# Seven-product query and key projections, whole PSUM bank pairs for turned tiles, weight sums on GpSimd, and a new order

## The chip, the cores and the metric

The kernel runs on one core of one Trainium2 chip. The metric is device time in microseconds, the lower the better. The engines are TensorE (PE), VectorE (DVE), ScalarE (ACT), GpSimd (POOL) and SyncE (SP); PEld is PE's weight load. All transfers are issued by SP.

## What is computed

Three layers follow each other, for B = 2 batches of S = 768 tokens, all in fp32:

```python
# 1. retention, 8 heads of 64
state = gamma * state + k_t v_t^T;  y_t = scale * q_t state
# 2. MLP on x = [y of all heads], 512 wide
xn = (x - mean) / sqrt(var + 1e-6) * g_ln
x = x + relu(xn @ w_ch1) @ w_ch2          # 512 -> 2048 -> 512
# 3. attention of 4 experts, head size 64, two of them chosen by token
logits = x @ w_gate; weights = softmax over the top 2
q, k, v = x @ wq[e], x @ wk[e], x @ wv[e]
out += weight[e] * (softmax(causal(scale * q k^T)) @ v @ wo[e])
```

## The kernel before

One program holds all three layers. Every step is a node with an engine (or several to choose from), a cost, and the buffers that it reads and writes. A planner in the kernel's own code (`Plan.issue`) simulates the engines with those costs, gives each buffer its place in SBUF or PSUM when its first step starts, and writes the instructions in the order so found. Where several steps are ready, the one with the lowest number goes first: the place in the code, a bias, and a value from a table (`RANK`). The names of the table are the labels set by `P.at`, such as "q_proj 1". So costs, ranks and buffer places together decide the order on each engine, and each engine then works its list in order.

The retention runs in 12 tiles of 128 tokens (`r_tile`, L581 to L669): scores on PE (L581), the mask on DVE (L587), the products with the values and the running state (L600, L610), the update of the state (L618), a turn by PE transposes (L422), mean and variance on DVE (L642), the normalised tile xn on ACT (L655), a second turn, and a split of x into a rounded part and a residue, of which the sum is the fp32 value. A matrix product is then three products: high by high, high by residue, residue by high. Weights come as 64-bit floats in pieces (`load_piece`), which ACT, POOL and DVE turn into two parts (`split_piece`, L685 to L719).

The MLP has 8 layers of 256 channels, called f. The first two take twelve matmuls of 128x384 for a channel block and 384 tokens (`m_h`, L766), the later six seven products instead of eight for a block of two by two (`m_h7`, L858). These need sums of weights (`w_sums`, L735 and L740) and of tokens (`x_sums`, L817 to L827), all split into two parts again. `m_c` (L788) multiplies with the second matrix and adds to xT on DVE (L794); its last layer writes x once more as high part and residue (L801, L804).

The attention begins with queries and keys (`q_proj`, L952: twelve matmuls for each of batch, token block j, matrix and half p), values and gates (`q_val`, L976). `a_scores` makes scores (L1047), mask and maximum (L1054), exponentials (L1062), the division (L1068, L1069) and, on POOL, the gated weights (L1076). `a_turn` transposes them by PE (L422) into PSUM and copies them out on ACT or DVE (L446), `a_value` multiplies with the values (L1117), `a_out` with wo (L1144).

PSUM has eight banks of 512 words. A turned tile lies in two neighbouring banks, half in each, and two turned tiles share such a pair: `pb` names six places in three pairs for the retention, `pc` four places in two pairs for the attention. Fillers (L529) are matmuls on constants that stand at the start, where PE would be idle.

## Time and profile before

| | |
|---|---|
| median of 3 runs | 443.25 us (442.27 to 444.95) |
| the profiled execution's own time | 442.45 us |
| its span in the trace | 440.7 us |
| granted PE clock, mean | 0.999 |

A busy share is the time in which an engine has an instruction in work, over the span or a stretch. A row of waits says for whose instruction an engine stood idle. Matmuls overlap, so a matmul's mean duration is longer than its pitch, the time from one start to the next.

### The profile page before, as it was taken

To read this page: it belongs to the slowest core of one execution; us is meant where nothing else is said; L and a number is where in the kernel's file an instruction comes from. 1 tells how busy PE (TensorE), PEld (TensorE's weight loads), DVE (VectorE), ACT (ScalarE), POOL (GpSimd) and SP (SyncE) were. 2 spreads that over 40 slices of the span, in tenths; PEclk is the share of its full clock that TensorE was granted. 3 is DMA by queue.
4 is the path that set the end of the run, shared out by engine and by line. 5 is a ranking of instruction groups with operands and counts; after the bars stand their busy time and mean duration, and the time that the engine had idled before them with its cause. 6 is when DMAs were issued, how large, how long until landed. Compare 5 with 4: busy or idle time off the path is not lost.

```text
span 440.7 us, 9076 instructions
## 1 busy us (share of the span) xinstructions
PE 429.4 (97%) x3546; PEld 402.4 (91%) x3546; DVE 309.8 (70%) x743; ACT 217.7 (49%) x460; POOL 212.0 (48%) x219
## 2 busy tenths in 40 slices
PE   9988999999999999999999999999999999999996
PEld 8877889999999999999999999999999877887765
DVE  2769978765778876868877655668556778667663
ACT  1568775342656346335353264234533666656552
POOL 2668865999999528117136054200401343422430
PEclk9999999999999999999999999999999999999999
DMA  8999432210322304104112002001100001001121
GB/s 288 328 337 345 133 109 84 97 49 1 106 86 92 101 0 143 50 1 136 54 59 88 1 1 96 1 0 55 48 1 1 1 12 39 2 0 49 50 97 49
DMA packets 11995, 35.18 MB, mean 80 GB/s; under 512 B 1840, under 2 KB 2480, under 8 KB 11952
## 3 DMA queue, kind: packets, MB, share of 16 engines
q1 hardware_dynamic: 11952, 34.60, 22.7%
q8 instruction: 28, 0.46, 0.4%
q14 instruction: 15, 0.12, 0.1%
HBM read 31.45 MB, written 3.15 MB: 79 GB/s over the span
## 4 chain that ended last, share of the span: by engine, by line
PE 90%; ACT 3%; DVE 2%; DMA 2%; POOL 1%; issue 1%; SPq 0%; POOLq 0%; DVEq 0%
PE ps L788 30%; PE ps L858 20%; PE ps L766 8%; PE ps L952 8%; PE ps L1117 4%; PE ps L976 4%; PE ps L422 4%; PE ps L1144 4%; PE ps L1047 3%; DMA raw<-in_w_dram 2%; PE ps L529 2%; PE ps L610 1%; PE ps L581 1%; ACT xn L655 1%; PE ps L600 1%
## 5 line engine op out<-in xcount | busy, mean ns | idle before, releaser
L788 PE MATMUL ps<-h,w 128*128 128x384 f32 x768 | 142.4, 335 | 0.0
L788 PEld LDWEIGHTS ps<-h,w 128*128 128x128 f32 x768 | 133.7, 188 | 0.7 <-DVE ps L798 0.3
L794 DVE TENSOR_TENSOR xT<-xT,ps 128x384 f32<-128x384 f32 x112 | 60.2, 550 | 30.6 <-PE ps L788 30.1
L1076 POOL TENSOR_SCALAR pr<-pr,sm,gate 128x384 f32<-128x384 f32 (+5 forms) x48 | 34.0, 718 | 77.9 <-DVE sm L1069 34.1
L719 POOL TENSOR_TENSOR w<-wy,w 128x512 fp32r<-128x512 f32 x26 | 34.0, 1319 | 38.1 <-PE ps L788 23.4
L858 PE MATMUL ps<-t,S 128*128 128x384 f32 x216 | 42.1, 334 | 0.0
L858 PEld LDWEIGHTS ps<-t,S 128*128 128x128 f32 x216 | 37.8, 188 | 0.0
L1062 ACT ACTIVATE pr<-pr,sm 128x384 f32<-128x384 f32 (+5 forms) x48 | 31.7, 663 | 9.9 <-DVE sm L1054 9.9
L766 PE MATMUL ps<-x,w 128*128 128x384 f32 x192 | 35.2, 337 | 0.0
L877 ACT ACTIVATE h<-ps 128x384 fp32r<-128x384 f32 x36 | 17.7, 490 | 32.9 <-PE ps L788 20.6
L766 PEld LDWEIGHTS ps<-x,w 128*128 128x128 f32 x192 | 33.2, 188 | 0.3
L685 ACT ACTIVATE wx<-raw 128x512 f32<-128x512 f32 x32 | 21.5, 671 | 23.8 <-DVE ps L692 16.0
L687 POOL TENSOR_SCALAR wx<-wx 128x512 f32<-128x512 f32 x32 | 20.0, 625 | 23.9 <-ACT wx L685 23.0
L867 ACT ACTIVATE u<-ps 128x384 f32<-128x384 f32 x36 | 17.5, 488 | 25.3 <-PE ps L858 16.6
L858 PE MATMUL ps<-x,w 128*128 128x384 f32 x144 | 28.6, 334 | 0.0
L689 DVE TENSOR_SCALAR ps<-wx 128x512 uint32<-128x512 uint32 x32 | 22.0, 688 | 6.4 <-POOL wx L687 6.1
L858 PEld LDWEIGHTS ps<-x,w 128*128 128x128 f32 x144 | 25.3, 188 | 0.0
L1054 DVE CUSTOM_DVE_ANT_0 pr<-ps,mask 128x384 f32<-128x384 f32 (+4 forms) x48 | 22.1, 495 | 3.2 <-PE ps L1047 2.2
L695 DVE SCALAR_TENSOR_TENSOR wy<-raw,ps 128x512 uint32<-128x512 uint32 x32 | 21.8, 683 | 2.3 <-POOL w L719 1.7
L879 DVE SCALAR_TENSOR_TENSOR h<-ps,h 128x384 fp32r<-128x384 f32 x36 | 19.4, 551 | 5.3 <-ACT h L877 5.2
L692 DVE SCALAR_TENSOR_TENSOR ps<-wx,ps 128x512 uint32<-128x512 uint32 x32 | 22.2, 695 | 1.1
L587 DVE TENSOR_TENSOR am<-ps,caus 128x512 f32<-128x512 f32 x24 | 15.5, 683 | 9.9 <-PE ps L581 9.9
(122 smaller groups left out, 822.7 us busy)
## 6 DMA issues: line engine op xcount, KB each, us to landing
raw<-in_w_dram SPq DMA_DIRECT2D x32, 512.0 KB, 3.4
kq<-in_kq_dram SPq DMA_DIRECT2D x11, 512.0 KB, 5.1
vk<-in_vk_dram SPq DMA_DIRECT2D x9, 512.0 KB, 5.5
out_dram<-ob SPq DMA_DIRECT2D x11, 256.0 KB, 2.0
vk<-in_vk_dram SPq DMA_DIRECT2D x4, 256.0 KB, 3.8
vraw<-in_wv_dram SPq DMA_DIRECT2D x1, 520.0 KB, 3.9
kq<-in_kq_dram SPq DMA_DIRECT2D x2, 256.0 KB, 5.2
mraw<-in_wk_dram SPq DMA_DIRECT2D x1, 512.0 KB, 4.6
```

Source lines behind the costliest of these rows:

```text
L689: DVE(0.69, lambda: dve.tensor_scalar(u32(z), u32(x), 4, 1, op0=OP.logical_shift_left, op1=OP.logical_shift_right), r=[x], w=[z])
L692: DVE(0.7, lambda: dve.scalar_tensor_tensor(u32(z), u32(x), 0x80000000, u32(z), op0=OP.bitwise_and, op1=OP.bitwise_or), r=[x, z], w=[z])
L695: DVE(0.7, lambda: dve.scalar_tensor_tensor(u32(y), words(0), 29, u32(z), op0=OP.logical_shift_right, op1=OP.bitwise_or), r=[raw, z], w=[y])
L719: POOL(1.3, lambda: pool.tensor_tensor(f32r(l), f32(y), f32(h), OP.subtract), r=[y, h], w=[l])
L766: pe.matmul(f32(pa, TB), lhsT=wt, rhs=blk(f32r(xt[b][j]))[:, k], start=(n == 0), stop=(n == 11))
L788: pe.matmul(f32(pa, TB), lhsT=wt, rhs=t, start=(n == 0), stop=(n == 5))
L794: DVE(0.55, lambda: dve.tensor_tensor(blk(f32(xt))[:, k], blk(f32(xt))[:, k], f32(pa, TB), OP.add), r=[pa] + [(xt, cc, w) for cc in range( ...
L858: pe.matmul(f32(pa, TB), lhsT=wt, rhs=t, start=(first and n == 0), stop=(n == 5), skip_group_check=True)
L952: pe.matmul(f32(pa, TB), lhsT=mw(n, lo, k, p * 128, (p + 1) * 128), rhs=blk(f32r(xt))[:, k], start=(i == 0), stop=(i == 11))
L1054: DVE(0.22 + wide * 1.04e-3, lambda ks=ks, n=n, z=z, SC=SC: dve.tensor_tensor_reduce(f32(PR[z])[:, ks], f32(SC[z])[:, :wide], f32(MASK)[:, ...
L1062: ACT(act_c(nk) + .18, lambda pr=pr, z=z: act.activation(f32(pr, nk), f32(pr, nk), AF.Exp, bias=f32(sm)[:, z:z + 1], scale=-1.0, accum_out ...
L1076: POOL(0.34 + nk * 0.84e-3, lambda pr=pr, z=z, e=e: pool.tensor_scalar(f32(pr, nk), f32(pr, nk), f32(sm)[:, 6 + z:7 + z], GT[b, j][:, cc, ...
```

## The change

- `pb` and `pc` now give a turned tile a whole pair of banks: three places for the retention, four for the attention (all eight banks). In the attention a tile holds up to six blocks instead of four. Scores and values may use all banks.
- The queries and keys of a batch are made by seven products of six matmuls instead of eight (`q_proj(b, n)`), as `m_h7` does. That takes sums of the blocks of wk and wq on POOL (`load_mw`), differences of token blocks, which POOL makes a second time with the final x (`x_sums(b, False)`), and steps that keep and add products (ACT, DVE). `m_c` copies the final x to xT for it (ACT).
- `w_sums` may no longer take DVE. The division's addition is done in two steps of one column.
- The running states of both batches count as one thing, so an update waits for the copy of the other batch's state too.
- Some regions of SBUF move (batch 0's queries, keys and values, the probability tiles), and every rank and some costs change.

```diff
-    "q_proj 1": (32, (-66, -79, -22, 88, -127, 8, 130, 119)),
+    "q_proj 1": (28, (-88, -100, -69, -116, -49, -91, -74, -142)),
...
-    PL["psa"] = banks[4:][::-1]
-    PL["ps1"] = banks[:4]
+    PL["psa"] = banks[::-1]
+    PL["ps1"] = banks
     PL["state"] = banks[:1]
 
...
-    PL["pb"] = [("P", 1024 * i + 256 * k, 256) for i in (1, 2, 3) for k in range(2)]
-    PL["pc"] = [("P", 1024 * i + 256 * k, 256) for i in (3, 2) for k in range(2)]
-
-    def two(b):
-        i, k = divmod(b.at[1], 1024)
-        return ps[:, 1024 * i:1024 * i + 1024].rearrange("p (h c) -> p h c", h=2)[:, :, k:k + 256]
+    PL["pb"] = [("P", 1024 * i, 1024) for i in (1, 2, 3)]
+    PL["pc"] = [("P", 1024 * i, 1024) for i in (3, 2, 1, 0)]
+
+    def two(b, n=256):
+        return view(b).rearrange("p (h c) -> p h c", h=2)[:, :, :n]
 
...
-            PE(0.47, upd, form="columns", r=[(vk, 1), vs] + (["first"] if i == 1 else []), w=[(STATE, b)] + (["first"] if i == 0 else []))
+            PE(0.47, upd, form="columns", r=[(vk, 1), vs], w=[STATE])
...
-            P.add({"V": 1.5, "G": 0.76} if f < ALONE else {"G": 0.75}, lambda e, i=i, p=p, q=q, op=op: (dve if e == "V" else pool).tensor_tensor(
+            P.add({"G": 0.75}, lambda e, i=i, p=p, q=q, op=op: (dve if e == "V" else pool).tensor_tensor(
...
         P.at = "m_c 5"
+        ACT(0.49, lambda: act.activation(blk(f32(xt))[:, k], f32(pa, TB), AF.Copy), r=[pa], w=[(xt, "k", k)])
+        P.at = "m_c 6"
         DVE(0.55, lambda: dve.tensor_tensor(blk(f32r(xl))[:, k], f32(pa, TB), blk(f32(xh))[:, k], OP.subtract),
-            r=[pa, (xh, "k", k)], w=[(xl, "k", k)] + (keys(xl) if k == 0 else []))
+            r=[pa, (xt, "k", k), (xh, "k", k)], w=[(xl, "k", k)] + (keys(xl) if k == 0 else []))
 
...
-    def x_sums(b):
+    def x_sums(b, own=True):
...
+        xs = {2: (0, 1), 0: (0, 0), 1: (1, 1), 3: (1, 0)}
+
+        def part(t, new):
+            if own or new:
+                return lambda: plain(tl[t]), [tl[t]]
+            kh, j = xs[t]
+            return lambda: f32(XT[b][j])[:, kh * TW:(kh + 1) * TW], [(XT[b][j], "k", 2 * kh + k) for k in range(2)]
+
+        for t, p, q, made in ((0, 2, 0, ()), (2, 1, 2, ()), (1, 1, 0, (0,)), (3, 3, 1, (1,))):
+            (xp, rp), (xq, rq) = part(p, p in made), part(q, q in made)
             P.at = "x_sums 2"
-            both(lambda en, t=t, p=p, q=q: en.tensor_tensor(plain(tl[t]), plain(tl[p]), plain(tl[q]), OP.subtract),
-                 [tl[p], tl[q]], [tl[t]])
+            both(lambda en, t=t, xp=xp, xq=xq: en.tensor_tensor(plain(tl[t]), xp(), xq(), OP.subtract), rp + rq, [tl[t]])
...
+        if n in ("wk", "wq"):
+            sh, sl = new("Sq"), new("Sq")
+            at = lambda i, m: f32(raw)[:, 512 * i:512 * i + 512].rearrange("p (k m c) -> p k m c", k=2, m=2)[:, :, m]
+            part = lambda i: plain(sl)[:, 256 * i:256 * i + 256].rearrange("p (k c) -> p k c", k=2)
+            for i, p, q, op in ((0, lambda: at(0, 1), lambda: at(1, 1), OP.add),
+                                (1, lambda: part(0), lambda: at(0, 0), OP.subtract),
+                                (2, lambda: at(0, 0), lambda: at(0, 1), OP.subtract),
+                                (3, lambda: at(1, 0), lambda: part(1), OP.subtract)):
+                P.at = "load_mw 4"
+                POOL(0.76, lambda i=i, p=p, q=q, op=op: pool.tensor_tensor(part(i), p(), q(), op), r=[raw], w=[sl])
+            P.at = "load_mw 5"
+            ACT(1.1, lambda: act.activation(f32r(sh), plain(sl), AF.Copy), r=[sl], w=[sh])
+            P.at = "load_mw 6"
+            POOL(2.41, lambda: pool.tensor_tensor(f32r(sl), plain(sl), f32(sh), OP.subtract), r=[sl, sh], w=[sl])
+            MW[n, "S"] = (sh, sl)
...
-    def q_proj(b, j, n, p):
-        cs = slice(j * TB, (j + 1) * TB)
-        pa = new("ps")
-        xh, xl = XH[b][j], XL[b][j]
-        for hf in range(2):
-            def mm(hf=hf):
-                i = 6 * hf
-                for k in (2 * hf, 2 * hf + 1):
-                    for lo, xt in ((0, xh), (0, xl), (1, xh)):
-                        pe.matmul(f32(pa, TB), lhsT=mw(n, lo, k, p * 128, (p + 1) * 128), rhs=blk(f32r(xt))[:, k],
-                                  start=(i == 0), stop=(i == 11))
+    def q_proj(b, n):
+        sh, sl = MW[n, "S"]
+
+        def product(pa, wn, xn, first):
+            h, l = (sh, sl) if wn[0] == "s" else MW[n][:2]
+            c0, step = (256 * int(wn[1]), 128) if wn[0] == "s" else ((512 if wn[0] == "y" else 0) + 128 * int(wn[1]), 256)
+            if xn[0] == "t":
+                xs = TH[b][int(xn[1])], TL[b][int(xn[1])]
+                xr, xat = list(xs), lambda k: tuple(f32r(t)[:, k * TB:(k + 1) * TB] for t in xs)
+            else:
+                kh, xs = int(xn[1]), (XH[b][int(xn[2])], XL[b][int(xn[2])])
+                xr, xat = xkeys(xs[0]) + xkeys(xs[1]), lambda k: tuple(blk(f32r(t))[:, 2 * kh + k] for t in xs)
+
+            def mm():
+                i = 0
+                for k in range(2):
+                    wh, wl = (f32r(t)[:, c0 + k * step:c0 + k * step + 128] for t in (h, l))
+                    xh, xl = xat(k)
+                    for wt, t in ((wh, xh), (wh, xl), (wl, xh)):
+                        pe.matmul(f32(pa, TB), lhsT=wt, rhs=t, start=(first and i == 0), stop=(i == 5), skip_group_check=True)
                         i += 1
             P.at = "q_proj 1"
-            PE(1.06, mm, r=list(MW[n][:2]) + xkeys(xh) + xkeys(xl) + ["seven"], w=[pa])
-        hi, lo = (QK[n, y, b, p] for y in range(2))
-        by = 0.125 if n == "wq" else 1.0
-        P.at = "q_proj 2"
-        ACT(0.485, lambda: act.activation(f32r(hi)[:, cs], f32(pa, TB), AF.Copy, scale=by), r=[pa], w=[(hi, j)])
-        P.at = "q_proj 3"
-        DVE(0.556, lambda: dve.scalar_tensor_tensor(f32r(lo)[:, cs], f32(pa, TB), by, f32(hi)[:, cs], op0=OP.mult, op1=OP.subtract),
-            r=[pa, (hi, j)], w=[(lo, j)])
+            PE(1.04, mm, r=[h, l] + xr + ["seven"], w=[pa])
+
+        def keep(pa):
+            u = new("uq")
+            P.at = "q_proj 2"
+            ACT(0.49, lambda: act.activation(f32(u), f32(pa, TB), AF.Copy), r=[pa], w=[u])
+            return u
+
+        def add(dst, pa, u):
+            P.at = "q_proj 3"
+            DVE(0.55, lambda: dve.tensor_tensor(f32(dst, TB), f32(pa, TB), f32(u), OP.add), r=[pa, u], w=[dst])
+
+        def out(src, p, j):
+            cs = slice(j * TB, (j + 1) * TB)
+            hi, lo = (QK[n, y, b, p] for y in range(2))
+            by = 0.125 if n == "wq" else 1.0
+            P.at = "q_proj 4"
+            ACT(0.485, lambda: act.activation(f32r(hi)[:, cs], f32(src, TB), AF.Copy, scale=by), r=[src], w=[(hi, j)])
+            P.at = "q_proj 5"
+            DVE(0.556, lambda: dve.scalar_tensor_tensor(f32r(lo)[:, cs], f32(src, TB), by, f32(hi)[:, cs], op0=OP.mult, op1=OP.subtract),
+                r=[src, (hi, j)], w=[(lo, j)])
+
+        pa, pb, pc = (new("ps") for _ in range(3))
+        product(pa, "a0", "x00", True)
+        c1 = keep(pa)
+        product(pb, "s1", "t1", True)
+        add(pb, pb, c1)
+        product(pa, "y0", "x10", False)
+        out(pa, 0, 0)
+        u2 = keep(pb)
+        product(pc, "s0", "t0", True)
+        product(pb, "s2", "t2", False)
+        u3 = keep(pb)
+        c22 = new("uq")
+        add(c22, pc, u3)
+        product(pb, "y1", "t3", False)
+        out(pb, 1, 0)
+        product(pc, "s3", "x11", False)
+        add(pc, pc, u2)
+        out(pc, 0, 1)
+        out(c22, 1, 1)
...
-            dve.tensor_scalar(m[:, 4:6], m[:, 2:4], 1e-9, None, op0=OP.add)
+            for z in range(2):
+                dve.tensor_scalar(m[:, 4 + z:5 + z], m[:, 2 + z:3 + z], 1e-9, None, op0=OP.add)
...
-            for s0 in range(0, len(slots), 4):
-                part = slots[s0:s0 + 4]
+            half = (len(slots) + 1) // 2 if len(slots) > 4 else len(slots)
+            for s0 in range(0, len(slots), half):
+                part = slots[s0:s0 + half]
...
+    x_sums(0, False)
     flush()
+    x_sums(1, False)
 
     def q_phase(b):
         q_alloc(b)
         for j in range(NB):
-            for n in ("wk", "wq"):
-                for p in range(2):
-                    q_proj(b, j, n, p)
-            P.bias += 20 * (b + 1)
             for t in range(TPB):
                 q_val(b, TPB * j + t)
             gates(b, j)
-            P.bias -= 20 * (b + 1)
+        for n in ("wk", "wq"):
+            q_proj(b, n)
```

By the orders, the 192 matmuls of L952 become 168 (L995), and 48 copies of turned probability tiles 40. PE has 2296 rows before and 2273 now, DVE 668 and 670, ACT 379 and 421, POOL 224 and 256.

Below stand three places of the order. Numbers in names are buffers and differ between the two programs; line numbers after the change are higher by 8 to 78.

POOL ahead of the projections, before: the residues of four weight matrices, then the first gated probabilities.

```order
L925 TENSOR_TENSOR wk_3218<-mraw_3176,wk_3208 128x1024
L925 TENSOR_TENSOR wq_3242<-mraw_3192,wq_3227 128x1024
L925 TENSOR_TENSOR wo_3565<-mraw_3518,wo_3555 128x1024
L925 TENSOR_TENSOR wv_3585<-vraw_3507,wv_3539 128x1040
L1219 MEMSET mask_3611 128x640
L1076 TENSOR_SCALAR pr_3641<-pr_3641,sm_3642,gate_72 128x384
```

And now: the differences of token blocks of batch 0 (t from xT), their residues (t from t, t), and batch 1's first ones, among the residues of wo and wv.

```order
L840 TENSOR_TENSOR t_1304<-xT_616,xT_140 128x768
L840 TENSOR_TENSOR t_1335<-xT_616,t_1304 128x768
L840 TENSOR_TENSOR t_1384<-xT_140,t_1335 128x768
L840 TENSOR_TENSOR t_1258<-xT_616 128x768
L845 TENSOR_TENSOR t_1453<-t_1304,t_1386 128x768
L845 TENSOR_TENSOR t_1469<-t_1335,t_1402 128x768
L845 TENSOR_TENSOR t_1443<-t_1384,t_1428 128x768
L840 TENSOR_TENSOR t_1502<-xT_764,xT_248 128x768
L845 TENSOR_TENSOR t_1425<-t_1258,t_1407 128x768
L943 TENSOR_TENSOR wo_3666<-mraw_3556,wo_3598 128x1024
L840 TENSOR_TENSOR t_1484<-xT_764 128x768
L943 TENSOR_TENSOR wv_3711<-vraw_3543,wv_3588 128x1040
```

Ten POOL steps now stand where the residues of wo and wv stood alone, and the products with sums on PE follow them.

POOL ahead of the first seven-product layer (f = 2), before: residues of weight pieces (L719, L710), token sums (L817, L821), one weight sum (L735) and the residue of the weight sums (L740).

```order
L817 TENSOR_TENSOR t_1579<-x_363,x_389 128x768
L710 TENSOR_TENSOR w_218_1595<-wy_1571,w_218_1595 128x256
L735 TENSOR_TENSOR sf_1604<-wy_1571 128x256
L719 TENSOR_TENSOR w_225_1625<-wy_1581,w_220_1601 128x512
L687 TENSOR_SCALAR wx_1627<-wx_1627 128x512
L817 TENSOR_TENSOR t_1639<-x_933,x_957 128x768
L821 TENSOR_TENSOR t_1579<-t_1518,t_1579 128x768
L740 TENSOR_TENSOR S_1677<-sf_1604,S_1665 128x1024
```

And now, up to the same residue (L748):

```order
L827 TENSOR_TENSOR t_1611<-x_389,x_407 128x768
L718 TENSOR_TENSOR w_222_1615<-wy_1593,w_222_1615 128x256
L743 TENSOR_TENSOR sf_1632<-wy_1593,wy_1613 128x256
L743 TENSOR_TENSOR sf_1632<-sf_1632,wy_1593 128x256
L743 TENSOR_TENSOR sf_1632<-wy_1593 128x256
L743 TENSOR_TENSOR sf_1632<-wy_1613,sf_1632 128x256
L695 TENSOR_SCALAR wx_1650<-wx_1650 128x512
L840 TENSOR_TENSOR t_1611<-t_1611,t_1529 128x768
L748 TENSOR_TENSOR S_1697<-sf_1632,S_1676 128x1024
```

All four weight sums (L743) now stand on POOL; before, three of them stood on DVE. From the first token sum to this residue POOL has 27 steps before and 33 now, 16 and 20 of them token sums.

SP at the start, before (kq holds a tile's keys and queries, vk its values and keys):

```order
L505 DMA vk_82<-in_vk_dram 128x512
L495 DMA kq_85<-in_kq_dram 128x1024
L495 DMA kq_90<-in_kq_dram 128x512 x2
L498 DMA tabV<-in_tabV_dram 128x48
L500 DMA caus<-in_caus_dram 128x128
L505 DMA vk_98<-in_vk_dram 128x1024
L513 DMA tab_5_103<-in_tabY_dram 128x512
L505 DMA vk_82<-in_vk_dram 128x512
L505 DMA vk_126<-in_vk_dram 128x1024
L515 DMA decay<-in_decay_dram 128x24
```

And now:

```order
L503 DMA kq_82<-in_kq_dram 128x512
L523 DMA decay<-in_decay_dram 128x24
L508 DMA caus<-in_caus_dram 128x128
L503 DMA kq_82<-in_kq_dram 128x512
L506 DMA tabV<-in_tabV_dram 128x48
L521 DMA tab_2_91<-in_tabY_dram 128x512
L548 DMA ident<-in_ident_dram 128x128
L513 DMA vk_96<-in_vk_dram 128x512
L552 DMA gln<-in_gln_dram 128x4
L503 DMA kq_103<-in_kq_dram 128x1024
L513 DMA vk_116<-in_vk_dram 128x1024
L513 DMA vk_96<-in_vk_dram 128x512
```

The first tile's keys and queries (kq_82, in two halves) now come first, tables between them, its values (vk_96) eighth. Before, the values of that tile came first and the keys of two tiles next.

## Rows read from the trace of the kernel before

**Rows 1.** The page: the span, and each engine's busy time, share and instructions.
```profile
span 440.7 us, 9076 instructions
PE 429.4 (97%) x3546; PEld 402.4 (91%) x3546; DVE 309.8 (70%) x743; ACT 217.7 (49%) x460; POOL 212.0 (48%) x219
```

**Rows 2.** Busy us by stage: PE, PEld, DVE, ACT, POOL; granted clock, DMA share, GB/s.
```profile
0.00:7.00 7.00, 5.95 (x30) 5.83 (x30) 0.17 (x2) 1.28 (x1) 0.20 (x4) 1.00 0.72 228
7.00:62.00 55.00, 51.10 (x879) 44.44 (x880) 43.68 (x99) 35.16 (x73) 40.39 (x50) 1.00 0.76 269
62.00:146.00 84.00, 84.00 (x536) 82.85 (x533) 62.93 (x118) 41.99 (x77) 76.39 (x61) 1.00 0.22 75
146.00:312.00 166.00, 166.00 (x958) 165.78 (x958) 119.14 (x217) 73.44 (x141) 55.57 (x55) 1.00 0.17 55
312.00:338.00 26.00, 26.00 (x176) 25.25 (x174) 15.26 (x54) 8.67 (x21) 6.77 (x5) 1.00 0.01 3
338.00:437.20 99.20, 96.38 (x981) 78.22 (x980) 68.20 (x254) 57.18 (x150) 32.67 (x46) 1.00 0.08 29
```

**Rows 3.** Waits of PE at L422: for whom, us, times, longest.
```profile
PE ps L422 <- DVE pt L446: 1.6, 3, 0.7
...
PE ps L422 <- ACT xn L655: 1.2, 1, 1.2
...
PE ps L422 <- ACT xc L664: 1.1, 2, 0.6
...
PE ps L422 <- ACT ptn L446: 0.7, 2, 0.4
...
PE ps L422 <- DVE mv L642: 0.4, 1, 0.4
```

**Rows 4.** PE's timeline: start us, us, line and operation, in the attention.
```profile
388.12 1.20 PE L952 MATMUL ps<-x,wk 128*128 128x384 f32 x6
...
389.16 1.20 PE L952 MATMUL ps<-x,wq 128*128 128x384 f32 x6
...
396.06 1.32 PE L952 MATMUL ps<-x,wk 128*128 128x384 f32 x6
...
397.31 1.52 PE L1117 MATMUL ps<-ptn,vv 128*64 128x256 f32 x16
```

**Rows 5.** Groups of instructions by line: busy us, mean ns of one, idle before.
```profile
L821 POOL TENSOR_TENSOR t<-t,t 128x768 f32<-128x768 f32 x8 | 15.0, 1876 | 0.3
...
L867 ACT ACTIVATE u<-ps 128x384 f32<-128x384 f32 x36 | 17.5, 488 | 25.3 <-PE ps L858 16.6 <-DVE ps L872 7.1 <-DVE ps L689 1.1
...
L872 DVE TENSOR_TENSOR ps<-ps,u 128x384 f32<-128x384 f32 x24 | 13.6, 565 | 8.9 <-PE ps L858 8.3 <-ACT x L801 0.5
...
L669 POOL TENSOR_TENSOR x<-xc,x 128x512 fp32r<-128x512 f32 x12 | 15.4, 1281 | 5.6 <-ACT x L667 5.6
...
L667 ACT ACTIVATE x<-xc 128x512 fp32r<-128x512 f32 x12 | 7.6, 631 | 0.3
...
L664 ACT ACTIVATE xc<-ps 128x512 f32<-128x512 f32 x12 | 7.1, 592 | 6.4 <-DVE mv L642 2.9 <-PE ps L422 2.0 <-POOL vs L571 1.5
...
L1068 DVE TENSOR_SCALAR sm<-sm 128x2 f32<-128x2 f32 x24 | 4.0, 168 | 4.1 <-ACT pr L1062 4.0
```

**Rows 6.** POOL's timeline from the first token sum to the weight residue.
```profile
82.35 3.66 POOL L817 TENSOR_TENSOR t<-x,x 128x768 f32<-128x768 f32 x2
...
120.17 2.39 POOL L740 TENSOR_TENSOR S<-sf,S 128x1024 fp32r<-128x1024 f32 x1
```

**Rows 7.** One line's instructions: ns min/median/max, starts, forms (L879, L735).
```profile
L879 DVE SCALAR_TENSOR_TENSOR h<-u,h x12: 548/556/1639, 135.8 to 305.1; 128x384 fp32r<-128x384 f32 x12
...
L735 POOL TENSOR_TENSOR sf<-wy x6: 732/740/971, 113.4 to 262.6; 128x256 f32<-128x256 f32 x6
```

**Rows 8.** PE's timeline at the start.
```profile
6.98 2.08 PE L581 MATMUL ps<-kq 64*128 64x128 f32 x32
...
9.64 1.09 PE L610 MATMUL ps<-am,vs 128*64 128x128 f32 x16
```

## What I expect

> **What bounds the kernel now.** I read the page first. Its span is 440.7 us, and TensorE (PE) is busy 97% of it while VectorE (DVE), ScalarE (ACT) and GpSimd (POOL) are at 70, 49 and 48% [rows 1]. An average over stages with different limits says little, so the next view is the busy time by stage [rows 2]. There the reader is to see three regimes. From 62 to 338 us PE has no idle time at all, at a granted clock of 1.00 (the 2.4 GHz level); 958 matmuls in 166 us are 173.3 ns each. In the first 62 us, the retention tiles, PE idles 1.05 + 3.90 us. From 338 us on, the attention, it idles 2.82 us of 99.2 beside a DVE that works 68.2 of them. The third view says what those idle times waited for: 5.0 us belong to one line, the transposes at L422, which wait for a copy or a statistic that reads an earlier turned tile out of PSUM, or for one that writes their own input [rows 3].
>
> So a matmul taken away is worth its whole pitch, wherever PE stays fed; a new wait on PE costs its whole length; and up to about 5 us of waits for turned tiles could go.
>
> **The change part by part. Products.** The projections of queries and keys were 192 matmuls of 128x384 (L952) and become 4 groups of seven products of six matmuls, 168. A group of six follows another after 1.04 us, 173.3 ns each [rows 4], so 24 fewer are **-4.16 us**. The groups that stand next to another operation take longer: 1.25 us from the start of such a six to the start of the next operation, 0.2 more [rows 4]. By the orders, PE changes its kind of operation 101 times before and 106 times in the change: 50 to 61 up to the end of the retention work, 51 to 45 after it. Those of the first stretch lie among waits, the six that fall away later would be worth up to 0.6 each way (0.2 for a pair).
>
> **What the products need first.** Per batch, POOL makes four differences of token blocks and four residues again, 16 steps of 1.88 us in all [rows 5], after the last addition to x. The first product with a sum stands 66 matmuls behind the last matmul that its difference needs: 66 x 0.173 = 11.4 us. The way there is a DVE addition of 0.57, an ACT copy of 0.49 [rows 5], and five POOL steps, 9.4 us, together 10.5. It fits by 0.9 us, so 0; if each engine hands over late, up to +2. The work beside it, 12 more ACT copies out of PSUM and 12 more DVE additions (0.49 and 0.57 each [rows 5]), falls where ACT works 8.7 and DVE 15.3 of 26 us [rows 2], and, for the second batch, in the attention: 0 there as long as DVE has the slack computed below. The two weight sums for it on POOL (8 steps of 0.74 and 2 residues) stand ahead of the block differences, at the end of a stage in which POOL works 55.6 of 166 us [rows 2]: 0.
>
> **Weight sums on POOL.** This is the one place where POOL is nearly full: 76.4 of 84 us between 62 and 146 [rows 2]. Before, the steps from the first token sum to the weight residue of the first seven-product layer took from 82.35 to 122.56 us, 40.2 us [rows 6]. In the new order the same stretch holds four more token sums (20 instead of 16, +7.5) and three weight sums of 0.74 more [rows 7] (+2.2): 49.9 us. It begins behind the last tile's transposes, after two ACT copies of 0.6 and a POOL step of 1.3 [rows 5], 2.7 with the hand-overs: 52.6. PE has 295 matmuls between those transposes and the first use of that residue, 51.1 us, and two small transposes, 51.7. So POOL comes 0.9 us late: I take **+0.8**, and 0 to +2.5 as bounds. The five sums taken from DVE save it some 4 us where PE waits for POOL, not DVE: 0.
>
> The two engines block each other, and this enters the bounds: the DVE step that reads u and h, both in SBUF, takes 548 ns at least, and 1639 at most, beside POOL [rows 7], while its median is 556. The Trainium skill (SBUF — State Buffer, Who interferes with whom) has the rule for it: a VectorE instruction with two SBUF inputs and a GpSimd instruction that reads SBUF exclude each other for a whole instruction. The trace agrees (1639 is 548 and most of a 1.88 us POOL step). By that rule the four new steps that make a residue of a sum held in SBUF would cost DVE up to 4 x 1.09 = 4.4 us amid POOL's new sums, and the five that leave DVE free POOL in the full stage.
>
> **Turned tiles.** A turned tile now owns two whole banks. In the retention there are three places instead of six. Before, PE waited there 1.2, 1.1 and 0.4 us for an earlier tile's reader [rows 3]. Fewer places speak for more such waits; that MLP matmuls stand between retention steps earlier in the new order (the first after 49 rows instead of 68) speaks for fewer. I take 0, between -2.7 (all of them gone) and +7.5 (eleven more of 0.68, their mean over four). In the attention the four places stay four, but each takes up to six blocks instead of four: 40 copies instead of 48. The waits there are 1.6 + 0.7 us [rows 3]; I take a quarter away, **-0.6**, between -2.3 and +3. The upper end is DVE: its 68.2 us stay, 24 divisions' extra steps of 0.17 (4.1) and six additions (3.4) come on top [rows 5], eight copies shrink; about 75 us in 95, 79% instead of 69%, with 24 filling matmuls fewer on PE.
>
> **The start.** The first tile's keys now head SP's queue and its values come eighth. The first scores began at 6.98 us for two tiles, the first product with values at 9.64 [rows 8]. Scores may start earlier, but of one tile only (1.04 us of work) until the values land: 0, between -2.6 (the stretch between the two rows) and +1.04.
>
> **Waits that are added.** The state of both batches is now one thing: an update must wait until the copy of the other batch's state has been read. Ten copies; in the new order other PE work stands between the updates, so 0. The rest (the second reader of a PSUM tile behind the first) lies on DVE and ACT, which have slack in those stages [rows 2].
>
> **Sum**, against the profiled execution's own 442.45 us (1.75 above its span, 0.8 below the median of the three runs): 442.45 - 4.16 + 0.8 - 0.6 = **438.5 us**. The three runs lie 2.7 us apart, so I don't add the 0.8. A change under 0.5% (2.2 us) can hardly be told from none here.
>
> **The rivals.**
> *The waits go too.* If the 2.3 us of the attention and most of the retention's go, and POOL is not late: 442.45 - 4.2 - 2.3 - 2 = 434. For it: those waits are for places in PSUM, which is what changes. Against: three places in the retention instead of six. The Trainium skill (Perfetto Trace Analysis, Identifying the Most-Contended Engine) would have weight loads, not matmuls, tell PE's headroom; by them the attention has 99.2 - 78.2 = 21 us of it [rows 2], not 2.8. The trace doesn't decide it, since its transposes and small matmuls load less.
>
> *POOL becomes the bound.* If its steps between 62 and 146 us run 5% longer, 80 busy us grow by 4, which PE gives back one for one, since it waits for POOL's sums at every product: 442.45 - 4.2 + 4 = 442. It decides from a PE idle time of 2 us in that stretch on. For it: no slack in my sum above. Against: two-operand DVE steps leave.
>
> *Slower.* The retention runs out of turned-tile places. If 16 of the 24 turned tiles wait 0.68 us more, +10.9: 449. From eleven on (+7.5) the kernel is slower than before by more than can be told from nothing: 442.45 - 4.0 + 7.5 = 446. For it: the three waits of that kind that there are already. Against: up to the first MLP matmul the new order has at most two tiles at a time between their two transposes, so a third place is there for the second turn.
>
> **Numbers.** Products pay and little else moves (436.5 to 440.5): 0.48. The waits go too: 0.18. POOL bounds, 440.5 to 444.5: 0.26, a third of it under 441.0. Slower: 0.08. So faster by over 0.5% 0.48 + 0.18 + 0.08 = 0.74, within 0.18, slower 0.08. The range 434.5 to 443.0 leaves out the slower case (0.08), a good third of the second (0.07) and the worst of POOL's (0.05).
>
> **What would show it.** Right: 168 matmuls at L995, 173 ns apart; PE idle of 0 to 2 us at 62 to 146 us, behind POOL's S; no PE wait on POOL's t steps before the projections; L430's waits in the attention below 2 us. Wrong: PE idle over 7 us before 62 us behind readers of turned tiles; DVE above 85% in the attention with PE waiting for it; first scores later than 7 us.

## The result, and the profile after

The changed kernel takes **445.66 us** (median of 20 runs, 443.78 to 448.18), the kernel before 442.94 beside it (20 runs, 441.52 to 445.36): a ratio of **1.0065, 95% interval 1.0045 to 1.0085**. I had forecast 438.5 and a gain. The profiled execution is 445.35 us, its span 443.5. Ratios leave out the executions more than 1.5% above the fastest of the same kernel: one of the twelve of e5_gates2, three of the twelve of e6_fill and of e11_dve.

The page of the changed kernel, its span, busy times and granted clock in 40 slices (answers to [rows 1]):

```profile
span 443.5 us, 9143 instructions
...
PE 430.5 (97%) x3522; PEld 402.3 (91%) x3522; DVE 310.9 (70%) x767; ACT 234.5 (53%) x493; POOL 256.2 (58%) x251
...
PEclk9699999999999999999999999999999899999999
```

24 matmuls fewer, and yet PE is busy 1.1 us longer: two slices of the clock, the second and one at 344 us, are below 9. Busy us by stage, with the clock in the third column from the end (answers to [rows 2]; then finer cuts):

```profile
7.00:62.00 55.00, 50.47 (x786) 43.82 (x786) 42.19 (x96) 35.26 (x71) 38.73 (x49) 0.94 0.83 289
62.00:146.00 84.00, 83.48 (x591) 80.76 (x588) 56.36 (x111) 42.16 (x74) 79.35 (x68) 1.00 0.22 68
...
312.00:338.00 26.00, 26.00 (x162) 25.74 (x161) 17.91 (x33) 19.61 (x40) 25.84 (x15) 1.00 0.12 44
338.00:440.00 102.00, 98.55 (x1001) 80.46 (x999) 77.82 (x311) 62.55 (x163) 39.99 (x52) 0.98 0.08 27
...
12.00:18.00 6.00, 6.00 (x63) 5.06 (x64) 2.41 (x6) 1.45 (x3) 1.87 (x3) 0.50 0.91 323
...
340.00:344.00 4.00, 1.11 (x10) 0.91 (x8) 3.90 (x7) 0.84 (x2) 3.58 (x2) 1.00 0.00 0
...
346.00:348.00 2.00, 2.00 (x12) 1.73 (x12) 1.53 (x9) 0.07 (x1) 0.00 (x0) 0.50 0.00 0
```

From 62 to 338 us PE idles 0.52 us in all; POOL is now busy 25.84 of 26 us before the attention, where it worked 6.77 [rows 2]. What PE waited for:

```profile
PE ps L1051 <- DVE ga L1063: 3.3, 1, 3.3
PE ps L618 <- POOL vs L579: 2.7, 1, 2.7
...
PE ps L796 <- DVE h L781: 0.5, 1, 0.5
PE ps L430 <- ACT xn L663: 0.5, 1, 0.5
PE ps L430 <- ACT xc L672: 0.4, 1, 0.4
```

The waits for turned tiles, 5.0 us before [rows 3], are 0.9. In their place stand two single stops, one at the start (the first weighted values) and one at the value products (L1051), which waits for a copy of four gate columns out of PSUM. DVE's timeline shows why that copy is late:

```profile
338.81 1.20 DVE L1082 TENSOR_TENSOR ga<-ga 128x48 f32<-128x48 f32 x1
339.93 0.20 DVE L1083 TENSOR_TENSOR ga<-ga 128x48 f32<-128x48 f32 x1
340.16 1.75 DVE L1084 TENSOR_TENSOR ga<-ga,before 128x48 f32<-128x48 f32 x1
341.94 1.73 DVE L1085 TENSOR_TENSOR ga<-ga 128x48 f32<-128x48 f32 x1
...
343.87 0.42 DVE L454 COPY vv<-ps 128x256 f32<-128x256 f32 x1
344.20 0.15 DVE L1063 COPY ga<-ps 128x4 f32<-128x4 f32 x1
...
347.17 0.21 DVE L1084 TENSOR_TENSOR ga<-ga,before 128x48 f32<-128x48 f32 x1
```

The same step on 48 numbers takes 1.75 us at 340.16 and 0.21 at 347.17. POOL's timeline beside it, then PE's:

```profile
338.08 1.86 POOL L840 TENSOR_TENSOR t<-xT,t 128x768 f32<-128x768 f32 x1
340.02 3.58 POOL L845 TENSOR_TENSOR t<-t,t 128x768 fp32r<-128x768 f32 x2
```

```profile
333.79 7.32 PE L1051 MATMUL ps<-wv,x 128*128 128x260 f32 x60
344.41 1.83 PE L1051 MATMUL ps<-wv,x 128*128 128x260 f32 x12 [3.30 <-DVE ga L1063]
```

DVE's gate steps end when POOL's token differences do. The copies that free PSUM stand behind them on DVE, so PE stops for 3.30 us. Afterwards the granted clock is at 0.50 (the 1.2 GHz level) for some 3 us, and the next 18 score matmuls take 3.42 us, which take 2.01 in the trace of e4_short (below), which has no such stop:

```profile
346.17 3.42 PE L1122 MATMUL ps<-qk,qk 64*128 64x384 f32 x18
```

```profile
341.24 2.01 PE L1125 MATMUL ps<-qk,qk 64*128 64x384 f32 x18
```

In the kernel before the gates took 0.21 us a step, at 329 to 335 us, with POOL at rest.

### The profile page after: what moved, and what is told of

It reads as the page before. It is cut to its first block, busy times and chain, and to the rows that moved or that the text cites. A ratio compares the mean times of both kernels' runs of the same rounds, so it can differ in the third digit from the quotient of the medians.

```text
span 443.5 us, 9143 instructions
## 1 busy us (share of the span) xinstructions
PE 430.5 (97%) x3522; PEld 402.3 (91%) x3522; DVE 310.9 (70%) x767; ACT 234.5 (53%) x493; POOL 256.2 (58%) x251
## 4 chain that ended last, share of the span: by engine, by line
PE 80%; POOL 9%; DVE 4%; ACT 3%; issue 2%; DMA 1%; SPq 1%; POOLq 0%; ACTq 0%; DVEq 0%
PE ps L796 25%; PE ps L876 20%; PE ps L995 7%; PE ps L1122 5%; PE ps L1196 4%; PE ps L1223 4%; PE ps L430 4%; PE ps L1051 3%; POOL t L827 3%; POOL t L840 3%; PE ps L589 2%; PE ps L618 2%; POOL t L845 2%; PE ps L774 2%; PE ps L626 1%
## 5 line engine op out<-in xcount | busy, mean ns | idle before, releaser
L802 DVE TENSOR_TENSOR xT<-xT,ps 128x384 f32<-128x384 f32 x112 | 61.2, 552 | 25.3 <-PE ps L796 25.0
L774 PEld LDWEIGHTS ps<-x,w 128*128 128x128 f32 x192 | 33.2, 188 | 0.3
L845 POOL TENSOR_TENSOR t<-t,t 128x768 fp32r<-128x768 f32 x16 | 29.2, 1842 | 0.2
```

Of the source, the lines that this page charges most:

```text
L774: pe.matmul(f32(pa, TB), lhsT=wt, rhs=blk(f32r(xt[b][j]))[:, k], start=(n == 0), stop=(n == 11))
L802: DVE(0.55, lambda: dve.tensor_tensor(blk(f32(xt))[:, k], blk(f32(xt))[:, k], f32(pa, TB), OP.add), r=[pa] + [(xt, cc, w) for cc in range( ...
L845: both(lambda en, t=t: en.tensor_tensor(f32r(tl[t]), plain(tl[t]), f32(th[t]), OP.subtract), [tl[t], th[t]], [tl[t]])
```

## The experiments

Theory A: in the projections, steps of DVE are kept waiting while POOL reads SBUF, the copies that free PSUM and are queued behind them come late, PE stops, and then it runs at a lower clock. The rivals stand in the expectations. Most edits leave the plan and every buffer's place alone and move single steps in the emitted order:

```diff
+        for key, other in BEHIND:
+            step = order.pop([n.at for n, e in order].index(key))
+            order.insert([n.at for n, e in order].index(other) + 1, step)
         for n, e in order:
             n.fn(e)
```

A step is named as in the code, with its count. Ratios are to the kernel before, which ran beside each. The changed kernel ran twice: 445.66 us above, with a ratio of 1.0065, and 444.10 (e7_again), with 1.0047; the gains below are given against both where it matters.

**The gates behind the first scores (e1_gates).**

```diff
+BEHIND = [(("gates 1", 0), ("a_scores 2", 0)), (("gates 2", 0), ("gates 1", 0)), (("gates 3", 0), ("a_scores 2", 1)),
+          (("gates 1", 1), ("a_scores 2", 2)), (("gates 2", 1), ("gates 1", 1)), (("gates 3", 1), ("a_scores 2", 3))]
```

> Only the order is changed, in one place: the two gate calculations of the first batch run on VectorE behind the first score steps instead of between the value copies. Theory A (small VectorE steps with two SBUF operands are held up by GpSimd's token differences, the PSUM copies queued behind them come late, TensorE stands still and its granted clock then halves): the wait of 3.30 us at the value products falls under 0.5 us and the half clock after it (0.50 in 346 to 348 of the changed kernel's trace, about 1.7 us lost) goes too, 4.5 to 5 us less than the changed kernel, so a ratio to the kernel before of 0.993 to 0.998. Rival (the wait is only pushed on: the scores' banks or GpSimd's multiplications by the gates wait in its place): 0 to 1.5 us less, ratio 1.003 or more.

Measured 442.11 us, ratio 0.9992 (0.9969 to 1.0015). By the ratios that is 0.7% less than the changed kernel, 3.2 us (2.4 us against e7_again), between the two expectations. The stop at the value products is gone, but the rival is partly right, by the waits of this kernel:

```profile
PE ps L1135 <- DVE sm L1142: 1.2, 1, 1.2
```

**The values earlier at the start (e2_start).**

```diff
+BEHIND = [(("load 4", 0), ("load 2", 0)), (("load 7", 0), ("load 6", 0)), (("load 8", 0), ("r_tile 1", 0))]
```

> Only the order is changed, at the start: the first half of the values is fifth in SP's queue instead of eighth, and GpSimd weights them before it scales the table. Theory A (TensorE's 2.72 us wait for the weighted values at 7.4 to 10.1 us is lost, and the half clock from 11.7 to 18 us that follows it costs about 3 us more): both go, 4.5 to 5.5 us less than the changed kernel, ratio to the kernel before 0.994 to 0.997. Rival (the transfers run one behind the other anyhow, so the next tile's keys and values are what is late next): 0 to 2.5 us less, ratio 1.001 to 1.0065.

Measured 445.24, ratio 1.0064 (1.0040 to 1.0088): no gain. The theory that this order gives back what the start costs fell. The wait for POOL shrank to 0.4 us, and the next transfer took it over:

```profile
PE ps L636 <- DMA vk<-in_vk_dram: 2.0, 1, 2.0
```

**Both orders (e3_both).** The two lists together.

> The two changes of order together. Theory A: they add up, 9 to 10.5 us less than the changed kernel, about 436 us, ratio to the kernel before 0.982 to 0.988. Rival: part of the two gains is the same slack in the last stage, or other waits fill in: 3 to 6 us less, ratio 0.993 to 0.9995.

Measured 442.53, ratio 1.0003 (0.9987 to 1.0019): what the gates alone give. It is 2.7 us less than the changed kernel by the ratios, just short of the rival's 3 to 6 us, and far from theory A's 9 to 10.5.

**POOL's last differences as zeros (e4_short).** The gates stay where they were. The last four low halves (the residues of batch 1's token differences) are written as zeros.

```diff
-            both(lambda en, t=t: en.tensor_tensor(f32r(tl[t]), plain(tl[t]), f32(th[t]), OP.subtract), ...)
+            if own or b == 0:
+                both(lambda en, t=t: en.tensor_tensor(f32r(tl[t]), plain(tl[t]), f32(th[t]), OP.subtract), ...)
+            else:
+                both(lambda en, t=t: en.memset(f32(tl[t]), 0.0), ...)
```

> The order of the changed kernel on every engine; GpSimd's four last subtractions of the second batch's token differences (1.86 us each, two SBUF operands) are replaced by writing zeros, so the low halves of those differences are left out of the output. Theory A: the gate steps on VectorE that took 1.75 and 1.73 us take 0.2 us, with nothing moved on VectorE, the wait of 3.30 us falls under 1 us and the half clock behind it goes; 3.5 to 5 us less than the changed kernel, ratio to the kernel before 0.994 to 0.999. Rival (it is the place and number of the gate steps ahead of the copies, not what GpSimd does): the wait stays over 2 us, ratio 1.003 or more.

Measured 439.83, ratio **0.9946** (0.9928 to 0.9965): by the ratios 1.2% less than the changed kernel, 5.3 us (4.5 us against e7_again), with every engine's order as there. DVE's timeline, and the windows of two stretches:

```profile
337.93 0.21 DVE L1087 TENSOR_TENSOR ga<-ga,before 128x48 f32<-128x48 f32 x1
338.18 0.21 DVE L1088 TENSOR_TENSOR ga<-ga 128x48 f32<-128x48 f32 x1
```

```profile
338.00:352.00 14.00, 14.00 (x99) 12.72 (x98) 11.86 (x59) 8.20 (x23) 4.14 (x7) 1.00 0.01 2
...
12.00:18.00 6.00, 5.32 (x98) 4.51 (x94) 3.61 (x8) 2.45 (x5) 1.84 (x3) 1.00 0.97 350
```

There is no stop and no fall of the clock there. So it is POOL's work and not the gates' place. The second row matters too: it is the same start, 2.4 us of waiting for the weighted values, and yet a clock of 1.00.

**The second gate later still (e5_gates2).** As the first, with the last three pairs behind `a_scores 2` 5, `gates 1` 1 and `a_scores 4` 0.

> As the first experiment, but the second of the two gate calculations stands three score steps later, behind the sixth, because in the first experiment VectorE's score steps came late and TensorE waited 1.2 us for a bank of scores. Theory A (what is lost in this stage is lost through VectorE's late release of banks and the clock that falls after the stop): the wait of 1.2 us goes as well; 4.5 to 5.5 us less than the changed kernel from the value products on, 440 to 441 us, ratio to the kernel before 0.992 to 0.997. Rival (GpSimd's multiplications by the later gates now come late and hold up the turns of the weights): a wait over 1 us at the first turns of the weights, ratio 0.998 to 1.002.

Measured 442.39, ratio 0.9992 (0.9976 to 1.0008): no better than the first. The ratio is the rival's, but its wait isn't there: the wait at the scores went, and one for the second batch's products came in its place, behind an ACT copy that waits for DVE's sums:

```profile
PE ps L1008 <- ACT uq L1016: 2.1, 1, 2.1
```

DVE idles between the value copies, where the gates were, and is short of time after them. One execution took 448.73 us.

**Fillers at the start (e6_fill).**

```diff
         for n, e in order:
-            n.fn(e)
+            for _ in range(6 if n.at == ("spin 1", 9) else 1):
+                n.fn(e)
```

> As e5_gates2, and TensorE runs five more products that nobody reads in its wait for the first weighted values (7.4 to 10 us); no transfer and no step is earlier. Theory B (at the start the wait itself costs nothing, since the next transfers would be waited for anyhow; what costs is the half clock at 11.7 to 18 us, which comes after the idle stretch): the granted clock stays at 1.00 through the first 20 us and the first seven-product layer begins 1.0 to 1.5 us earlier, ratio to e5_gates2 about 0.997. Rival 1 (the half clock has nothing to do with the idle stretch): half clock as before, no difference. Rival 2 (the added products delay the first products with the values): 0.3 us or more slower.

Measured 442.62 (441.22 to 449.18), ratio 1.0000 (0.9972 to 1.0028): no difference from e5_gates2 that can be told. In its trace the clock stays at 1.00 from 7 to 20 us, where e5_gates2's has 0.74, as theory B expected; e13_nofill comes back to it. The trace happens to be one of the long executions, 449.18 us, and shows something else, in DVE's, POOL's and PE's timelines:

```profile
326.85 5.69 DVE L1031 SCALAR_TENSOR_TENSOR qk<-uq,qk 128x384 fp32r<-128x384 f32 x1
```

```profile
326.10 1.89 POOL L854 TENSOR_TENSOR t<-xT 128x768 f32<-128x768 f32 x1
327.90 2.48 POOL L957 TENSOR_TENSOR wv<-vraw,wv 128x1040 fp32r<-128x1040 f32 x1
330.30 1.83 POOL L859 TENSOR_TENSOR t<-t,t 128x768 fp32r<-128x768 f32 x1
332.04 0.66 POOL L1312 MEMSET mask<- 128x640 f32 x1
```

```profile
334.44 2.29 PE L1009 MATMUL ps<-t,wq 128*128 128x384 f32 x6 [4.10 <-ACT uq L1017]
```

This is the low half that is made from a sum in SBUF, one of the four steps that I had priced. It loses its turn to three POOL steps in a row and gets it when POOL only writes.

**The changed kernel once more (e7_again).**

> The changed kernel once more, beside the others on one chip: ratio to the kernel before 1.004 to 1.009. Every theory expects the wait of about 3.3 us at the value products and the half clock behind it; theory B leaves open whether the clock falls in the first 20 us of this execution, and expects the first seven-product layer at 124.0 us if it does not and 125.3 us if it does.

Measured 444.10, ratio 1.0047 (1.0030 to 1.0065), stop of 3.2 us. The same low half in this trace, on DVE and beside it POOL:

```profile
327.05 1.54 DVE L1017 SCALAR_TENSOR_TENSOR qk<-uq,qk 128x384 fp32r<-128x384 f32 x1
```

```profile
326.30 1.87 POOL L840 TENSOR_TENSOR t<-xT 128x768 f32<-128x768 f32 x1
328.10 2.79 POOL L943 TENSOR_TENSOR wv<-vraw,wv 128x1040 fp32r<-128x1040 f32 x1
```

Here DVE gets its turn at the first boundary, and POOL's next step is 0.3 us longer (2.79, beside 2.48 above).

**Eight products again (e8_eight).** `q_proj` and its calls are those of the kernel before, without the token differences and weight sums for it.

> The changed kernel with one part undone: the query and key projections with eight products as before, without the token differences and weight sums for them; the planner orders it anew, so other places move too. From the sum of the prediction (24 products of 173.3 ns) and theory A (5.0 us lost through GpSimd's token differences): 4.2 us more and 5.0 us less, so 0.5 to 1.5 us less than the changed kernel, about 444.5 us, ratio 1.002 to 1.005, with the gate steps at 0.2 us each. Rival (the seven products do save and the loss is elsewhere): 3 to 5 us more than the changed kernel, ratio 1.013 or more.

Measured 451.33, ratio 1.0207 (1.0188 to 1.0226): 7.2 more than the changed kernel on this chip. That is the rival's side, but how much of it the seven products save this run can't say: planned anew, it has waits of its own at the last MLP matmuls and the first projections (1.7 and 1.6 us for DVE's x). Its gate steps take 0.21 us, and there POOL is idle.

**POOL busy, but not reading (e9_busy).** As the run with zeros, three writes instead of one.

```diff
-                both(lambda en, t=t: en.memset(f32(tl[t]), 0.0), ...)
+                both(lambda en, t=t: [en.memset(f32(tl[t]), 0.0) for _ in range(3)], ...)
```

> As e4_short, but each of the four replaced GpSimd steps is three writes of zeros, so that GpSimd is busy as long as in the changed kernel (3 times 0.73 us in place of 1.86 us) and reads nothing in them; the low halves of the second batch's token differences are left out of the output, as there. Theory A (VectorE's steps with two SBUF operands are kept waiting by GpSimd's reading steps): the gate steps that fall beside the writes take 0.2 us, the wait at the value products stays under 1 us, ratio to the kernel before 0.994 to 0.998, as e4_short up to what the later token differences cost. Rival (any busy GpSimd, or its late end, is enough): gate steps of 1 us and more, a wait of 2.5 us or more, ratio 1.003 or more.

Measured 442.15, ratio 0.9995 (0.9971 to 1.0019): more than I had put it at. The low half lost its turn here too, in the trace (3.93 us, with 2.3 us of PE's waiting). At the gates the theory held. DVE, then POOL:

```profile
340.56 0.21 DVE L1087 TENSOR_TENSOR ga<-ga,before 128x48 f32<-128x48 f32 x1
```

```profile
338.01 4.62 POOL L848 MEMSET t<- 128x768 f32 x6
```

A POOL that is busy writing for 4.62 us delays the gates by nothing, so it is its reading.

**One SBUF operand (e10_one).** The four low halves are a product with zero, so they are left out.

```diff
+            if src.kind == "uq":
+                DVE(0.556, lambda: dve.tensor_scalar(f32r(lo)[:, cs], f32(src, TB), 0.0, None, op0=OP.mult), ...)
+                return
```

> The changed kernel, in which the four low halves that are made from a sum in SBUF (two SBUF operands) are a product of that sum with zero instead (one SBUF operand); these low halves are left out of the output. Open is what makes single executions of these kernels 2 to 4 us longer than others; e6_fill's trace shows one of these four steps at 5.69 us, three GpSimd steps long, and TensorE waiting 4.10 us behind it. Theory A: no execution of that kind is left, so the spread of the times shrinks from 4.4 us (443.8 to 448.2) to about 2 us, and the four steps take 0.6 us or less; the gates' wait of 3.3 us stays, median 0 to 1.5 us less than the changed kernel, ratio 1.001 to 1.006. Rival (the long executions have another cause): the same spread, and the same ratio of 1.005 to 1.0065.

Measured 446.07 (443.35 to 447.15), ratio 1.0066 (1.0043 to 1.0090). The theory in the form that I had given it, two operands, fell:

```profile
326.82 6.27 DVE L1018 TENSOR_SCALAR qk<-uq 128x384 fp32r<-128x384 f32 x1
```

This step has one operand, from SBUF to SBUF, and it waits as long. PE then waits 4.5 us behind it and comes late to the value products, where its stop is 0.6 us. Undisturbed, this step takes 0.35 us, where the two-operand step takes 0.55.

**Two differences on DVE (e11_dve).** Nothing is left out here; the fillers are those of e6_fill.

```diff
-            both(lambda en, t=t: en.tensor_tensor(
+            both(lambda en, t=t: (dve if not own and b == 1 and t in (1, 3) else en).tensor_tensor(
+BEHIND = [(("gates 1", 0), ("q_val 3", 3)), (("gates 2", 0), ("gates 1", 0)), (("gates 3", 0), ("q_val 3", 5)),
+          (("x_sums 4", 13), ("q_val 3", 4)), (("gates 1", 1), ("a_scores 2", 1)), (("gates 2", 1), ("a_scores 3", 1)),
+          (("gates 3", 1), ("a_scores 2", 4)), (("x_sums 4", 15), ("a_scores 2", 5))]
```

> A complete kernel: the last two low halves of the second batch's token differences go from GpSimd to VectorE, so that GpSimd is done about 3.7 us earlier; the first gate calculation then runs between the value copies as in the changed kernel, the second behind the scores' second and fifth step; five products that nobody reads fill TensorE's first wait, as in e6_fill. Theory A: the wait at the value products and the wait of 1.2 us at the scores both go, at the price of two more VectorE steps of about 1 us each; 4 to 6 us less than the changed kernel, ratio to the kernel before 0.989 to 0.996. Rival (VectorE is by now the engine that is short of time in this stage): a wait of 1 to 3 us behind VectorE's sums of the second batch, ratio 0.997 to 1.002.

Measured 446.11, ratio 1.0020 (0.9982 to 1.0059), in two groups: five executions at 440.5 to 442.6 us, seven at 445.5 to 448.4. The ratio is the rival's. The trace is one of the lower group: theory A's two waits are gone, the first low half takes 1.55 us, and 1.2 us of PE's waiting behind DVE's sums is left, as the rival had it.

**The two low halves when POOL is done (e12_c22).** To the list of e11_dve came these (and `gates 3` 1 behind them); the second sum got an SBUF place of its own, and one copy of values went from DVE to ACT:

```diff
+          (("q_proj 5", 3), ("a_scores 2", 4)), (("q_proj 5", 7), ("q_proj 5", 3)),
```

> A complete kernel: e11_dve, and the first batch's two low halves that are made from a sum in SBUF run on VectorE behind the fifth score step, when GpSimd reads nothing (the second sum has an SBUF place of its own for it; one value copy goes to ScalarE). e11_dve's executions fall into two groups, five at 440.5 to 442.6 us and seven at 445.5 to 448.4. Theory A (the upper group is the executions in which the first of these low halves loses its turn to three GpSimd steps in a row, as in e6_fill and e10_one at 5.69 and 6.27 us): no execution over 444 us, all at 440 to 443, ratio to the kernel before 0.994 to 0.999. Rival (the upper group has another cause): again half of the executions over 445 us, ratio about 1.002.

Measured 441.12 (440.05 to 444.10), ratio 0.9984 (0.9965 to 1.0003). The upper group is gone, but for one execution 0.1 us over the line, as theory A has it; e13_nofill, with the same order, has none above 443.86 in twelve. The copy on ACT came with the low halves, so they are not the only difference.

**The same without fillers (e13_nofill).**

> As e12_c22 without the five products that fill TensorE's first wait. Theory B (these products keep the granted clock up after the start): the clock falls to 0.5 in some stretch of the first 20 us and the time is 1 to 1.5 us more than e12_c22. Rival (the fall of the clock at the start comes and goes by itself, as the changed kernel's two traces, 0.74 and 0.87, and e4_short's, 1.00, with the same start, suggest): no difference over 0.5 us.

Measured 442.42 (440.17 to 443.86), ratio 0.9993 (0.9973 to 1.0013). The medians differ as theory B has it, within overlapping intervals; but the trace shows a clock of 1.00 from 7 to 20 us without a filler, and e14_order's, which has them, one of 0.72 from 12 to 18. So the clock can stay full without fillers and fall with them: theory B fell in that form. Whether they make the fall rarer stays open: the clock over the span, as a mean of twelve executions, is 0.998 in e12_c22 and 0.993 here, but 0.995 in e6_fill and 0.996 in e5_gates2.

**VectorE's order once more (e14_order).** The list of e12_c22, with these in place of two of its pairs:

```diff
+          (("q_proj 3", 6), ("a_scores 2", 5)), (("gates 3", 1), ("q_proj 3", 6)), (("x_sums 4", 15), ("a_scores 2", 7)),
```

> A complete kernel: e12_c22 with VectorE's order changed once more between 346 and 351 us, where e12_c22's TensorE still waits 0.61 us for a bank of scores and 1.21 us behind VectorE's sum for the second batch: the sixth score step and that sum now stand ahead of the last gate steps, and the low half of the token differences that is needed last stands behind the eighth score step. Theory A (after the port waits, what is left of the loss in this stage is VectorE's order): both waits go, 1.5 to 1.8 us less than e12_c22, about 439.4 us, ratio to the kernel before 0.992 to 0.996. Rival (VectorE has no slack here, and the work put back holds up the turns of the weights): a wait of about 1 us at a turn, no difference from e12_c22 over 0.5 us.

Measured **439.82** (439.21 to 441.18), ratio **0.9932** (0.9905 to 0.9959): faster than the kernel before, and than the changed kernel, whose ratios are 1.0065 and 1.0047. It holds more than the change does: the fillers, and steps moved from POOL to DVE and from DVE to ACT. Theory A expected both waits to go; in this stage 0.6 us of PE's waits are left:

```profile
PE ps L1073 <- DVE sm L1151: 0.6, 1, 0.6
```

## Why the prediction was wrong

Two steps failed, each put at 0, and a gain that I had put too low hid part of it.

**The first step that failed** is "What the products need first", which put the token differences ahead of the projections at 0, with +2 at most. It asked when POOL's sums are ready, and that was right: PE waited for none. It didn't ask what POOL's reading does to DVE meanwhile. I had the rule (the Trainium skill, SBUF — State Buffer, Who interferes with whom) and used it on the four steps that are new; the gates, which the change doesn't touch, I did not count, though they stand on DVE ahead of copies that free PSUM. From the start of the last seven-product group of the MLP to the end of the span (300.30 to 443.5) the changed kernel takes 143.2 us, the run with zeros 138.2 (from 299.01): **5.0 us** for the blocked gates and the clock after them.

The kernel before takes 141.5 us from that group on (from 299.21), but its work there is less. Up to that group the counts of PE's matmuls, before and after, differ in one row:

```profile
L788 PE MATMUL ps<-h,w 128*128 128x384 f32 x702 | 130.4, 335 | 0.0
```

```profile
L796 PE MATMUL ps<-h,w 128*128 128x384 f32 x678 | 125.4, 335 | 0.5 <-DVE h L781 0.5
```

The new order leaves 24 more of these matmuls behind that point, 4.16 us at 173.3 ns. For equal work the last stage gained 2.5 us in the changed kernel (143.2 - 4.16 - 141.5), 7.5 in the run with zeros and 6.5 in the last kernel (139.2, from 299.64). The sum gave -4.8 there.

**The second step that failed** is "The start", put at 0, with +1.04 at most, and with it what I put at 0 in the retention behind it. PE's first scores began at 4.90 us instead of 6.98 [rows 8], and its wait for the weighted values then was 2.72 us. At the last seven-product group the changed kernel is 1.1 us behind the kernel before in one trace, 0.0 in the other (299.18), and 0.2 ahead in the run with zeros; with the 24 matmuls that are still to do there it is **5.2, 4.1 and 4.0 us** behind. The clock of 12 to 18 us (0.50, 0.81, 1.00) goes with the difference between these. Estimated with the matmuls' mean pitches in the kernel before, about half of the 4.0 us in the run with zeros is lost by 62 us, the rest from there to 125 us. Of the 4.0, 2.2 us are more idle time of PE, 0.5 of it behind DVE (below). The rest is time in which PE was busy; the eleven more changes of operation in the retention and the joined state, both put at 0, lie there too, and no run separates them. The expectations of e2_start and e3_both had the size of this loss about right, but the two orders gave none of it back. What it hangs on stays open.

**By luck** 438.5 would nearly have been the time of the run with zeros (439.83): it lost 3.2 us more than the sum on the way to that group and gained 2.7 more behind it. In the changed kernel the way there cost 4.4 us more than the sum, and the stage behind it gained 2.3 less: together the miss (445.35 for 438.5).

**A size that was off**: "up to 4 x 1.09 us" for the four steps, from a step blocked once [rows 7]. Beside POOL steps in a row it has no such bound: 5.69 and 6.27 us, at one stroke. The step stands ahead of the additions and copies that PE's next products need, so it was on the path after all (4.1 and 4.5 us of PE's waiting). This is what makes the long executions of e6_fill and e11_dve, as far as e12_c22 shows. In both traces of the changed kernel the step took 1.5 us; that its own executions of 447 to 448 us have this cause isn't shown.

**Products, -4.16**: the groups of the projections are busy 33.2 us (L995) where they were 37.1 (L952), -3.9. Right.

**POOL late, +0.8**: this was about 0.2. PE idles 0.52 us from 62 to 146 us, but for DVE's h (L781), behind ACT, and not for POOL. POOL's residue ended at 129.45, and the first product with it began at 129.68, 0.2 us after its turn (126.38 and 18 pitches):

```profile
127.05 2.40 POOL L748 TENSOR_TENSOR S<-sf,S 128x1024 fp32r<-128x1024 f32 x1
```

```profile
126.38 3.46 PE L796 MATMUL ps<-h,w 128*128 128x384 f32 x18
129.68 2.24 PE L876 MATMUL ps<-t,S 128*128 128x384 f32 x12
```

So the rival "POOL becomes the bound" fell in its place; but POOL did become what decides, 200 us later.

**Turned tiles**: the retention waited 0.9 us instead of 2.7 [rows 3], the attention not at all instead of 2.3 (2.8 with two small waits that the rows leave out). Better than the 0 and -0.6 that I took; the rival "slower" by that way fell. In the attention the transposes are also busy 0.9 us less (14.9 for 15.8); with these waits (2.8) and the products (3.9) that makes up the 7.5 us of the run with zeros. In the retention the gain isn't seen in the time, since more was lost there.

## What to carry to other kernels

When a change gives one of VectorE and GpSimd more work on SBUF, list every step of the other in the same stretch that may need the shared port, the old and the tiny ones too, and ask what stands behind each in its queue. Such a step is best put where the other engine is idle or, if it reads two operands, only writes; otherwise its result can cost as many of the other's steps as stand in a row (three here). A stop that is removed from the path at the start is worth only what the next transfer leaves. And when two orders are compared up to a point in their traces, count the work done up to it: here 24 matmuls beyond that point hid 4.16 us.

## What the hardware showed that I had not expected

- The gate step of 0.21 us took 1.75 us beside POOL's steps. The Trainium skill (SBUF — State Buffer, Who interferes with whom) says that the engine that issues first holds the shared port for the whole instruction and the other fully blocks. The trace agrees, and shows more: the one that waits doesn't always come next. The low half took 1.54 us with one POOL step waited for, 5.69 and 6.27 with three.
- A DVE step with one SBUF operand waited 6.27 us. The Trainium skill (SBUF — State Buffer, Who interferes with whom) has copies, casts and `tensor_scalar` among the operations that can enter a two-port mode and then contend; I had used only its sentence on two inputs.
- POOL's writes of zeros (4.62 us) held up no gate step. The Trainium skill (SBUF — State Buffer, Who interferes with whom) has it so for steps with two SBUF inputs, and the trace agrees.
- The granted clock was 0.50 for 6 us in one execution of the changed kernel and 0.81 on average in another, after the same stop of 2.7 us; in the other runs without fillers it was 0.50 to 1.00 in the same 6 us, in the four with them 0.72 to 1.00. What decides it stays open.
